# Four column groups of h side by side in the first chunk, paired transposes of x, and a later tanh, in a feed-forward kernel with its gradients

## The chip, the cores and the metric

One core of a Trainium2 chip runs the whole program. The metric is device time in microseconds (us), of the slowest core, which here is the only one. Before the change the time was 321.61 us, the median of 3 runs (321.59 to 321.71).

## The reference, cut to what matters

```python
B, S, D, F = 1, 2048, 640, 1536            # bfloat16
def _fwd_reference(x, w1, w2):
    h = jnp.einsum("bsd,df->bsf", x, w1)
    h = _silu(h)
    out = jnp.einsum("bsf,fd->bsd", h, w2)
    return out
# reference(): the output, and by jax.vjp the gradients of x, w1 and w2 for grad_out
```

The kernel does six products of the same size: h, the gradient at h ("g"), two products back to 640 columns ("out" and the gradient of x), and the two weight gradients. Each is 240 matmuls of 128x128 weights by 512 columns.

## The kernel before

The rows are worked in four chunks of 512. Only the start of the first chunk is touched by the change. Four 128-row tiles of x are loaded and transposed by TensorE through PSUM (the memory that takes TensorE's results); w1 is loaded in pieces, in the order of the columns that the first groups need; then twelve column groups of h follow, each of five matmuls (one for each 128-row slice of w1). Matmuls on a constant ("warm") precede, so that TensorE is busy while the loads run. After h comes the stage with w2.

```python
load_x_tile(nc.sync, 0); load_x_tile(nc.scalar, 1)         # 160 KB each
load_x_tile(nc.sync, 2); load_x_tile(nc.scalar, 3)
for lo, hi in ((0, 2), (2, DT)):                           # 128 KB, 192 KB: columns 0 to 255
    nc.sync.dma_start(out=w1_nat[:, lo:hi, 0:FH], in_=w1_v[:, lo:hi, 0:FH])
load_w1(FH, FC)                                            # 320 KB: columns 256 to 511
for fc in range(1, NFC):
    load_w1(fc * FC, (fc + 1) * FC)                        # 640 KB each
# ... (w2, transposed loads)
def pe_x_tile(xT, st):                                     # one tile of x, 5 transposes
    for lo, hi, copy in ((0, DS, nc.vector.tensor_copy), (DS, DT, nc.scalar.copy)):
        tp = ps_h.tile([P, hi - lo, P], dt_in, name="tp", tag="hp")
        for dt_ in range(lo, hi):
            nc.tensor.transpose(tp[:, dt_ - lo, :], x_nat[:, st, dt_ * P:(dt_ + 1) * P], ident[:])
        copy(out=xT[:, lo:hi, st * P:(st + 1) * P], in_=tp[:])

for st in range(STC):
    pe_x_tile(xT_next, st)
for i in range(NFILL):                                     # 4 fillers, behind the transposes
    nc.tensor.matmul(wp[:, 0:P], lhsT=ident[:], rhs=x_nat[:, STC - 1, 0:P], start=True, stop=True)

def h_group(ft, xT, aT, ghT):
    hp = ps_h.tile([P, SC], FP32, name="hp")               # one of 8 PSUM buffers
    for dt_ in range(DT):
        nc.tensor.matmul(hp[:], lhsT=w1_nat[:, dt_, ft * P:(ft + 1) * P], rhs=xT[:, dt_, :],
                         start=(dt_ == 0), stop=(dt_ == DT - 1))
    nc.scalar.activation(aT[:, ft, :], hp[:], ACT.Silu)
    # ... tanh of hp on ScalarE, then two VectorE steps
```

## Time and profile before

| what | before | view |
|---|---|---|
| time, 3 runs | 321.59 to 321.71 us | run times |
| time of the profiled run | 322.23 us (span 320.5) | run times, page |
| TensorE busy | 98% | page, part 1 |
| first h matmul | 6.48 us | timeline of PE |
| first matmul of the w2 stage | 19.43 us | timeline of PE |

From the page, the busy time of the engines and the chain that ended last (by engine, then by line; L161 is h, L196 the w2 stages). "PEld" is the weight loads, which overlap PE.

```profile
...
PE 314.0 (98%) x1477; PEld 145.9 (46%) x1506; DVE 101.8 (32%) x179; ACT 78.6 (25%) x142; POOL 0.7 (0%) x6
...
PE 97%; DMA 1%; issue 1%; ACT 0%; SPq 0%; DVE 0%; DVEq 0%
PE hp L196 32%; PE hp L180 16%; PE hp L286 16%; PE hp L161 16%; PE hp L334 15%; DMA x_nat<-in_x_dram 1%; PE hp L316 1%; ACT xT L149 0%; PE tp L148 0%; SPq L123 0%; DVE g_2366 L327 0%; DVEq L327 0%
...
```

From the timeline of TensorE, merged: start in us, length in us, line, operation, tiles, and in brackets the idle time before it and what ended it. L96 is the warm matmuls, L148 the transposes, L154 the fillers, L161 h, L196 the w2 stage.

```profile
...
0.78 2.93 PE L96 MATMUL wp<-const-bfloat16-1.0 128*128 128x128 bf16 x26 [0.78 <-PEq L362]
3.62 0.74 PE L148 MATMUL tp<-ident,x_nat 128*128 128x128 bf16 x10
5.32 0.73 PE L148 MATMUL tp<-ident,x_nat 128*128 128x128 bf16 x10 [0.96 <-DMA x_nat<-in_x_dram]
5.88 0.39 PE L154 MATMUL wp<-x_nat,ident 128*128 128x128 bf16 x4
6.48 13.11 PE L161 MATMUL hp<-xT,w_nat 128*128 128x512 bf16 x58 [0.21 <-ACT xT L149]
19.43 4.91 PE L196 MATMUL hp<-aT,w_nat 128*128 128x512 bf16 x22
```

All idling of TensorE lies ahead of 6.48 us, and the h stream then runs without a bracket. (A count of 58 and not 60 means two records missing in the trace.) From the waits of TensorE: total us, number, longest.

```profile
...
PE tp L148 <- DMA x_nat<-in_x_dram: 1.0, 1, 1.0
PE wp L96 <- PEq L362: 0.8, 1, 0.8
PE hp L161 <- ACT xT L149: 0.2, 1, 0.2
```

There is no fourth line: in the whole span TensorE waits three times.

### The profile page before, as it was taken

What the parts mean: (1) busy time and instruction counts of PE and PEld (TensorE: products, weight loads), DVE (VectorE), ACT (ScalarE), POOL (GpSimd) and SP (SyncE); (2) the same over time, 40 slices, a digit from 0 to 9 for tenths busy, and PEclk for the clock granted to TensorE, in tenths of its full rate; (3) what the DMA queues carried; (4) which work ended last, traced back from release to release, by engine and by line L of the source; (5) the groups of instructions that cost most, each with busy time, mean ns of one, the idle gap of its engine ahead of it and who ended that gap; (6) DMA issues with size and microseconds to landing.
All of it is one profiled execution on the core that took longest, in us unless ns stands there. A gap on an engine that the chain in (4) does not pass through costs nothing.

```text
span 320.5 us, 3556 instructions
## 1 busy us (share of the span) xinstructions
PE 314.0 (98%) x1477; PEld 145.9 (46%) x1506; DVE 101.8 (32%) x179; ACT 78.6 (25%) x142; POOL 0.7 (0%) x6
## 2 busy tenths in 40 slices
PE   7999999999999999999999999999999999999996
PEld 5444444444444444444444444444444444444443
DVE  1871551477510087810147741000000100001001
ACT  3960001555201255411054520110100001001100
POOL 0000000000000000000000000000000000000000
PEclk9999999999999999999999999999999999999999
DMA  8999999999699884392445079819999999995011
GB/s 246 316 192 209 254 265 253 320 271 277 215 229 336 203 237 122 118 319 66 127 159 141 2 254 268 217 25 293 262 240 263 249 203 343 251 281 181 33 49 35
DMA packets 149264, 66.69 MB, mean 208 GB/s; under 512 B 112640, under 2 KB 149248, under 8 KB 149248
## 3 DMA queue, kind: packets, MB, share of 16 engines
q1 hardware_dynamic: 148960, 66.13, 80.8%
q10 hardware_dynamic: 288, 0.33, 0.3%
q8 instruction: 12, 0.20, 0.2%
q14 instruction: 4, 0.03, 0.0%
HBM read 9.18 MB, written 28.97 MB: 119 GB/s over the span
## 4 chain that ended last, share of the span: by engine, by line
PE 97%; DMA 1%; issue 1%; ACT 0%; SPq 0%; DVE 0%; DVEq 0%
PE hp L196 32%; PE hp L180 16%; PE hp L286 16%; PE hp L161 16%; PE hp L334 15%; DMA x_nat<-in_x_dram 1%; PE hp L316 1%; ACT xT L149 0%; PE tp L148 0%; SPq L123 0%; DVE g_2366 L327 0%; DVEq L327 0%
## 5 line engine op out<-in xcount | busy, mean ns | idle before, releaser
L161 PE MATMUL hp<-xT,w_nat 128*128 128x512 bf16 x232 | 56.4, 379 | 0.6 <-ACT xT L149 0.2
L180 PE MATMUL hp<-goT,w2T 128*128 128x512 bf16 x238 | 56.8, 379 | 0.1
L196 PE MATMUL hp<-aT,w_nat 128*128 128x512 bf16 x235 | 52.2, 379 | 0.3
L196 PE MATMUL hp<-ghT,w1T 128*128 128x512 bf16 x235 | 52.2, 379 | 0.3
L286 PE MATMUL hp<-a_blk,go_nat 128*128 128x512 bf16 x236 | 51.8, 379 | 0.2
L334 PE MATMUL hp<-gh_blk,x_nat 128*128 128x512 bf16 x219 | 48.2, 379 | 0.3
L204 ACT ACTIVATE oT<-hp 128x512 bf16<-128x512 f32 x24 | 14.3, 597 | 110.0 <-PE hp L196 110.0
L168 ACT ACTIVATE aT<-hp 128x512 bf16<-128x512 f32 x48 | 28.7, 597 | 31.7 <-PE hp L161 31.7
L196 PEld LDWEIGHTS <-w_nat 128*128 128x128 bf16 x240 | 23.5, 98 | 28.3
L180 PEld LDWEIGHTS <-w2T 128*128 128x128 bf16 x240 | 23.5, 98 | 28.3
L286 PEld LDWEIGHTS <-go_nat 128*128 128x128 bf16 x240 | 23.5, 98 | 28.3
L161 PEld LDWEIGHTS <-w_nat 128*128 128x128 bf16 x240 | 23.4, 98 | 28.4 <-issue 0.4
L196 PEld LDWEIGHTS <-w1T 128*128 128x128 bf16 x240 | 23.4, 98 | 28.4
L206 DVE CAST oT<-hp 128x512 bf16<-128x512 f32 x16 | 11.1, 692 | 78.0 <-PE hp L196 78.0
L187 DVE SCALAR_TENSOR_TENSOR ghT<-ghT,hp 128x512 bf16<-128x512 bf16 x48 | 32.5, 682 | 7.3 <-PE hp L180 7.3
L334 PEld LDWEIGHTS <-x_nat 128*128 128x128 bf16 x224 | 21.9, 98 | 26.4
L173 DVE SCALAR_TENSOR_TENSOR ghT<-aT,v 128x512 bf16<-128x512 bf16 x48 | 33.0, 688 | 0.6
L172 DVE TENSOR_SCALAR v<-t 128x512 bf16<-128x512 f32 x48 | 20.5, 427 | 29.2 <-ACT t L170 29.2
L170 ACT ACTIVATE t<-hp 128x512 f32<-128x512 f32 x48 | 28.4, 591 | 0.0
L296 DVE CAST g2T<-hp 128x512 bf16<-128x512 f32 x7 | 4.8, 692 | 46.1 <-PE hp L286 46.1
L294 ACT ACTIVATE g2T<-hp 128x512 bf16<-128x512 f32 x8 | 4.8, 598 | 47.0 <-PE hp L286 40.7
L343 ACT ACTIVATE g_2140<-hp 128x512 bf16<-128x512 f32 x1 | 0.6, 597 | 13.6 <-DMA out_dram<-g_2077 13.6
(33 smaller groups left out, 29.3 us busy)
## 6 DMA issues: line engine op xcount, KB each, us to landing
aT_scr<-aT SPq DMA_DIRECT2D x4, 1536.0 KB, 6.7
ghT_scr<-ghT SPq DMA_DIRECT2D x4, 1536.0 KB, 8.0
out_dram<-o_sb SPq DMA_DIRECT2D x8, 640.0 KB, 3.4
oT_scr<-oT SPq DMA_DIRECT2D x4, 640.0 KB, 3.9
go_nat<-in_grad_out_dram SPq DMA_DIRECT2D x4, 640.0 KB, 8.1
gxT_scr<-oT SPq DMA_DIRECT2D x4, 640.0 KB, 4.7
w_nat<-in_w_dram SPq DMA_DIRECT2D x2, 960.0 KB, 10.9
x_nat<-in_x_dram SPq DMA_DIRECT2D x3, 640.0 KB, 7.8
```

The costliest lines, as they stand in the source:

```text
L161: nc.tensor.matmul(hp[:], lhsT=w1_nat[:, dt_, ft * P:(ft + 1) * P], rhs=xT[:, dt_, :], start=(dt_ == 0), stop=(dt_ == DT - 1),)
L168: nc.scalar.activation(aT[:, ft, :], hp[:], ACT.Silu)
L170: nc.scalar.activation(t[:], hp[:], ACT.Tanh, scale=0.5)
L172: nc.vector.tensor_scalar(out=v[:], in0=t[:], scalar1=-0.5, scalar2=0.5, op0=ALU.mult, op1=ALU.add)
L173: nc.vector.scalar_tensor_tensor(out=ghT[:, ft, :], in0=aT[:, ft, :], scalar=1.0, in1=v[:], op0=ALU.subtract, op1=ALU.mult)
L180: nc.tensor.matmul(gp[:], lhsT=w2T[:, dt_, ft * P:(ft + 1) * P], rhs=goT[:, dt_, :], start=(dt_ == 0), stop=(dt_ == DT - 1),)
L187: nc.vector.scalar_tensor_tensor(out=ghT[:, ft, :], in0=ghT[:, ft, :], scalar=1.0, in1=gp[:], op0=ALU.add, op1=ALU.mult)
L196: nc.tensor.matmul(op_[:], lhsT=w_all[:, ft, dt_ * P:(dt_ + 1) * P], rhs=rhs_all[:, ft, :], start=(ft == 0), stop=(ft == FT - 1),)
L204: nc.scalar.activation(oT[:, dt_, :], op_[:], ACT.Copy)
L206: nc.vector.tensor_copy(out=oT[:, dt_, :], in_=op_[:])
L286: nc.tensor.matmul(gp[:], lhsT=go_nat[:, st, dt_ * P:(dt_ + 1) * P], rhs=a_blk[:, st, :], start=(st == 0), stop=(st == ST - 1),)
L334: nc.tensor.matmul(gp[:], lhsT=x_nat[:, st, dt_ * P:(dt_ + 1) * P], rhs=gh_blk[:, st, :], start=(st == 0), stop=(st == ST - 1),)
```

## The change

The intent is to start the h stream earlier. Blocks of x are transposed for two tiles at once and copied block by block, so that the first 128-row block of all 512 rows is complete first. The first four groups then run side by side: slice 0 of w1 for groups 0 to 3, slice 1 for groups 0 to 3, and then what is left, group by group. This needs slice 0 of 512 columns first, so w1's first loads are cut by rows and not by columns, and the second one is issued from ScalarE's queue. The fillers move between the pairs in the source; in the built program they stand ahead of all transposes. Tanh of a group follows silu of the group three later, so that silu isn't held up when groups finish close together.

```diff
-        for lo, hi in ((0, 2), (2, DT)):
-            nc.sync.dma_start(out=w1_nat[:, lo:hi, 0:FH], in_=w1_v[:, lo:hi, 0:FH])
-        load_w1(FH, FC)
+        for eng, lo, hi in ((nc.sync, 0, 1), (nc.scalar, 1, 2), (nc.sync, 2, DT)):
+            eng.dma_start(out=w1_nat[:, lo:hi, 0:FC], in_=w1_v[:, lo:hi, 0:FC])
 ...
-        for st in range(STC):
-            pe_x_tile(xT_next, st)
+        def pe_x_pair(xT, st):
+            for dt_ in range(DT):
+                tp = ps_h.tile([P, 2, P], dt_in, name="tp", tag="hp")
+                for q in range(2):
+                    nc.tensor.transpose(tp[:, q, :], x_nat[:, st + q, dt_ * P:(dt_ + 1) * P], ident[:])
+                copy = nc.scalar.copy if dt_ % 2 else nc.vector.tensor_copy
+                copy(out=xT[:, dt_, st * P:(st + 2) * P], in_=tp[:])
+        pe_x_pair(xT_next, 0)
         for i in range(NFILL):
-            nc.tensor.matmul(wp[:, 0:P], lhsT=ident[:], rhs=x_nat[:, STC - 1, 0:P], ...)
+            nc.tensor.matmul(wp[:, 0:P], lhsT=warm, rhs=warm, start=True, stop=True)
+        pe_x_pair(xT_next, 2)
 ...
+        def h_first(xT, aT, ghT):                    # KM = 2, FB = 4, LAG_G = 3
+            hps = []
+            for ft in range(FB):
+                hps.append(ps_h.tile([P, SC], FP32, name="hp"))
+            for dt_ in range(KM):
+                for ft in range(FB):
+                    h_mm(hps[ft], ft, xT, dt_, dt_ + 1)
+            for i in range(FT + LAG_G):
+                if i < FT:
+                    if i < FB:
+                        h_mm(hps[i], i, xT, KM, DT)
+                    else:
+                        hps.append(ps_h.tile([P, SC], FP32, name="hp"))
+                        h_mm(hps[i], i, xT, 0, DT)
+                    silu_a(i, hps[i], aT)
+                if i >= LAG_G:
+                    silu_grad(i - LAG_G, hps[i - LAG_G], aT, ghT)
 ...
             if c == 0:
-                for ft in range(FT):
-                    h_group(ft, xT, aT, ghT)
+                h_first(xT, aT, ghT)
```

More of the change, by code (lines that the diff above doesn't have):

```diff
@@ L44 @@
     NFC = F // FC
+    FB = FC // P
     LAG = 2
+    LAG_G = 3
+    KM = 2
     NWARM = 26
@@ L114, in load_goT @@
             return goT
-        FH = FC // 2
         xT_next = xpool.tile([P, DT, SC], dt_in, name="xT")
@@ L140, with h_mm @@
         nc.sync.dma_start_transpose(out=w1T[:], in_=w1[:, :])
-        DS = 3
-        def pe_x_tile(xT, st):
-            for lo, hi, copy in ((0, DS, nc.vector.tensor_copy), (DS, DT, nc.scalar.copy)):
-                tp = ps_h.tile([P, hi - lo, P], dt_in, name="tp", tag="hp")
-                for dt_ in range(lo, hi):
-                    nc.tensor.transpose(tp[:, dt_ - lo, :], x_nat[:, st, dt_ * P:(dt_ + 1) * P], ident[:])
-                copy(out=xT[:, lo:hi, st * P:(st + 1) * P], in_=tp[:])
-        for st in range(STC):
-            pe_x_tile(xT_next, st)
-        for i in range(NFILL):
-            nc.tensor.matmul(
-                wp[:, 0:P], lhsT=ident[:], rhs=x_nat[:, STC - 1, 0:P], start=True, stop=True
-            )
-        def h_group(ft, xT, aT, ghT):
-            hp = ps_h.tile([P, SC], FP32, name="hp")
-            for dt_ in range(DT):
+        def pe_x_pair(xT, st):
[6 more added lines that the diff above has]
+        pe_x_pair(xT_next, 0)
+        for i in range(NFILL):
+            nc.tensor.matmul(wp[:, 0:P], lhsT=warm, rhs=warm, start=True, stop=True)
+        pe_x_pair(xT_next, 2)
+        def h_mm(hp, ft, xT, lo, hi):
+            for dt_ in range(lo, hi):
                 nc.tensor.matmul(
@@ L167, in h_group, with silu_a, silu_grad @@
                 )
+        def silu_a(ft, hp, aT):
             nc.scalar.activation(aT[:, ft, :], hp[:], ACT.Silu)
+        def silu_grad(ft, hp, aT, ghT):
             t = tpool.tile([P, SC], FP32, name="t")
@@ L175, in h_group @@
             )
+        def h_group(ft, xT, aT, ghT):
+            hp = ps_h.tile([P, SC], FP32, name="hp")
+            h_mm(hp, ft, xT, 0, DT)
+            silu_a(ft, hp, aT)
+            silu_grad(ft, hp, aT, ghT)
+        def h_first(xT, aT, ghT):
[15 more added lines that the diff above has]
+                    silu_grad(i - LAG_G, hps[i - LAG_G], aT, ghT)
         def g_group(ft, goT, ghT):
@@ L277 @@
         g2T_v = g2T_scr[:].rearrange("(dt p) f -> p dt f", p=P)
-        FB = FC // P
         k = 0
```

## The prediction

> **What bounds the kernel now.** TensorE. The page gives PE 98% busy; the chain of waits is 97% PE. In the timeline the first h matmul starts at 6.48 us; from there weight loads follow every 0.216 us to the end, with no gap over 0.24 us (1440 x 0.216 = 311 us, of a span of 320.5). The waits view has only three PE waits, all in the first 6.5 us: 0.8 at the start barrier, 1.0 for x, 0.2 for the last transposed copy. Besides, there are about 3 us of closing copy and store. So the change can only move the start of the h stream, or break its density.
>
> **The start today.** x tiles 0 and 1 land at 3.57 and 3.74 us, tiles 2 and 3 at 5.27 and 5.50. Ten transposes at a 56 ns pitch follow each pair. The last VectorE copy (3 blocks, 0.36 us) ends at 6.33, the last ScalarE copy at 6.46. The first w1 pieces land at 5.78, 6.43 and 7.39: none is late.
>
> **What the change does.**
> 1. Transposes pair two x tiles per 128-row block, block 0 first: x tile 3 lands 5.50, block 0 is transposed by about 5.77, its copy of 256 columns (estimate 0.29 us, from the 0.36 us of 384) done at about 6.10. Block 4's copy ends at about 6.5, as today, but is needed only 8 matmuls (1.73 us) after the start.
> 2. Four groups side by side: the same 240 matmuls, of which the first need only w1's first slice.
> 3. w1's first two slices (128 KB each) are issued on two queues. The Trainium skill, "DMA: Bandwidth & Descriptors", section "Issuing engines are not separate DMA queues", says such queues share the same 16 engines and interleave. So slice 0 shares bandwidth with slice 1: by bytes in front of it (estimate from today's landings: 768 KB by 5.78, 960 KB by 6.43) it lands near 6.1, about when block 0 is ready. The rest (1280 KB, 7.4 us) is needed at about 7.95. Thin, but it holds.
> 4. The four fillers are scheduled before the transposes (order of the built program), ending near 3.8; this doesn't delay the second pair.
> 5. Tanh trails silu by three groups. ScalarE needs 1.08 us per group, PE 1.08. The first four groups finish 0.65 us apart, so tanh catches up later. Eight PSUM buffers cover it. Worth nothing by itself: ScalarE never stalled PE.
>
> **On the critical path.** Only the start: from 6.48 to about 6.2-6.3 us (block 0 copied, slice 0 landed, 0.1 us of wait and weight load). The gain is 0.2 us, below 0.1%. Everything after shifts as a block.
>
> **Predicted:** 321.38 us, range 321.05 to 321.75; faster by over 2%: 0.003, within 2%: 0.99, slower: 0.007.
>
> **Shown right or wrong by:** the first h matmul in the timeline at 6.2-6.3; its releaser a w1 slice or a VectorE copy; no PE gap among the first 60 h matmuls; the span minus that start unchanged at 314.0.
>
> **What would make it wrong.** (a) Slice 0 or x tile 3 lands later, as queues share the engines: no gain. (b) The w1 rest lands after 7.95 and opens a gap. (c) The clock: "TensorE: Matmul & The Clock Gate", Part 1, tells of a clock that halves after idle windows. Today's clock record goes to full at 3.67 us and stays; losing it would add up to 1.7 us (half speed over one 3.4 us window, an estimate from that page). (d) PSUM is freed too late, as tanh lags: gaps at groups 8-11.

## The result

The changed kernel took 322.26 us (median of 4 runs, 321.92 to 322.62), beside 321.66 us before (median of 4, 321.59 to 321.77). The ratio is 1.0019, with a 95% interval of 1.0001 to 1.0036: the same, by a limit of 2%, and outside the predicted range of 321.05 to 321.75. (Ratios are the mean time of one kernel's runs over that of the other's of the same rounds, so not quite the ratio of the medians quoted.)

From the page of the changed kernel, the same lines. Line numbers moved: h is L158 now, the w2 stages are L221.

```profile
...
PE 314.9 (98%) x1477; PEld 147.0 (46%) x1506; DVE 101.7 (32%) x181; ACT 77.7 (24%) x142; POOL 0.7 (0%) x6
...
PE 96%; DMA 2%; issue 1%; SPq 0%; DVE 0%; DVEq 0%
PE hp L221 32%; PE hp L309 16%; PE hp L205 16%; PE hp L158 16%; PE hp L357 15%; DMA w_nat<-in_w_dram 2%; PE hp L339 1%; SPq L125 0%; SPq L132 0%; DVE g_2370 L350 0%; DVEq L350 0%
...
```

A load of w1 ("DMA w_nat") has come into the chain with 2% of the span; x has left it. From the timeline of TensorE (L153 fillers, L147 transposes, L158 h, L221 the w2 stage):

```profile
...
3.50 0.63 PE L153 MATMUL wp<-const-bfloat16-1.0 128*128 128x128 bf16 x4
3.93 2.29 PE L147 MATMUL tp<-ident,x_nat 128*128 128x128 bf16 x20
6.05 1.89 PE L158 MATMUL hp<-xT,w_nat 128*128 128x512 bf16 x7
8.58 11.40 PE L158 MATMUL hp<-xT,w_nat 128*128 128x512 bf16 x51 [0.64 <-DMA w_nat<-in_w_dram]
19.81 4.48 PE L221 MATMUL hp<-aT,w_nat 128*128 128x512 bf16 x20
```

The stream does start earlier, at 6.05 us against 6.48. But after eight matmuls (one record missing) it stops, and goes on at 8.58. The bracket says 0.64 us only, because the end of a matmul is drawn later than the time at which the next could start. At the pace of 0.216 us for each matmul, the ninth was due at 6.05 + 8 x 0.216 = 7.78; it came 0.80 us late. From the waits of TensorE:

```profile
...
PE wp L99 <- PEq L385: 0.8, 1, 0.8
PE hp L158 <- DMA w_nat<-in_w_dram: 0.6, 1, 0.6
```

The ninth matmul is the first that needs the 384 KB load with slices 2 to 4. From the list of DMA issues of the changed kernel, that load alone: line, queue, count, size, us from issue to landing.

```profile
...
w_nat<-in_w_dram SPq DMA_DIRECT2D x1, 384.0 KB, 6.4
```

It was issued at 2.12 us and landed 6.4 us later, at 8.53. In the kernel before, the load with the same number of bytes in front of it and in it (1280 KB with x) is this one:

```profile
...
w_nat<-in_w_dram SPq DMA_DIRECT2D x1, 320.0 KB, 4.8
```

It was issued at 2.63 us and landed at 7.39, more than a microsecond earlier, and was not needed until the eleventh matmul. The first reading was thus case (b) of the prediction's list, "the w1 rest lands after 7.95 and opens a gap". That is true of this run. Whether it is the cause of the difference is another question, and it took repeats to see it.

### The profile page after: what moved, and what is told of

Read it like the earlier page. It is cut to its first block, busy times and chain, and to the rows that moved or that the text cites. A ratio compares the mean times of both kernels' runs of the same rounds, so it can differ in the third digit from the quotient of the medians.

```text
span 320.9 us, 3558 instructions
## 1 busy us (share of the span) xinstructions
PE 314.9 (98%) x1477; PEld 147.0 (46%) x1506; DVE 101.7 (32%) x181; ACT 77.7 (24%) x142; POOL 0.7 (0%) x6
## 4 chain that ended last, share of the span: by engine, by line
PE 96%; DMA 2%; issue 1%; SPq 0%; DVE 0%; DVEq 0%
PE hp L221 32%; PE hp L309 16%; PE hp L205 16%; PE hp L158 16%; PE hp L357 15%; DMA w_nat<-in_w_dram 2%; PE hp L339 1%; SPq L125 0%; SPq L132 0%; DVE g_2370 L350 0%; DVEq L350 0%
## 5 line engine op out<-in xcount | busy, mean ns | idle before, releaser
L158 PE MATMUL hp<-xT,w_nat 128*128 128x512 bf16 x238 | 56.9, 379 | 0.7 <-DMA w_nat<-in_w_dram 0.6
L221 PE MATMUL hp<-ghT,w1T 128*128 128x512 bf16 x235 | 52.2, 379 | 0.3
L221 PE MATMUL hp<-aT,w_nat 128*128 128x512 bf16 x235 | 52.2, 379 | 0.3
L167 ACT ACTIVATE aT<-hp 128x512 bf16<-128x512 f32 x48 | 29.9, 625 | 33.4 <-PE hp L158 33.4
L158 PEld LDWEIGHTS <-w_nat 128*128 128x128 bf16 x240 | 23.4, 98 | 29.0 <-DMA w_nat<-in_w_dram 1.1
L221 PEld LDWEIGHTS <-w1T 128*128 128x128 bf16 x240 | 23.5, 98 | 28.3
L221 PEld LDWEIGHTS <-w_nat 128*128 128x128 bf16 x240 | 23.5, 98 | 28.3
L171 ACT ACTIVATE t<-hp 128x512 f32<-128x512 f32 x48 | 29.8, 625 | 0.0
L368 DVE CAST g_2081<-hp 128x512 bf16<-128x512 f32 x1 | 0.7, 692 | 9.7 <-PE hp L357 9.7
```

Source lines behind the costliest of these rows:

```text
L171: nc.scalar.activation(t[:], hp[:], ACT.Tanh, scale=0.5)
L221: nc.tensor.matmul(op_[:], lhsT=w_all[:, ft, dt_ * P:(dt_ + 1) * P], rhs=rhs_all[:, ft, :], start=(ft == 0), stop=(ft == FT - 1),)
```

## The experiments

These theories were put against each other. T0: the first profile of before was a late sample, so the prediction was anchored wrongly. T1: each load of w1 has a deadline, the matmul that first reads it; the change moves the deadline of the last 384 KB from the eleventh matmul to the ninth. T2: two queues with slices of w1 at once make the transfers lag. T3: the moved fillers, and the time at which the clock of TensorE goes to full, make the start late. T4: the trailing tanh holds something up. Where the texts speak of "303.0 us", the start of the w2 stage was taken at its first weight load, some 0.2 us ahead of its first matmul, which is used below. T-numbers, KM and LAG_G are as above. The runs were made in five groups, each with fresh or shared runs of before on the same chip.

### Both kernels again

No edit.

> The kernel before, once more, for a second profile of its start and for the noise. Theory T0 (the first profile was a late sample: 322.23 us, when the timed runs were 321.6): x tile 2 lands near 4.5 us and not 5.27, the h stream starts at 5.8 to 5.9 us and not 6.48, and the span is near 319.8. Rival (profiling itself adds 0.6 us): the start is at 6.4 to 6.5 again. Ratio 1.000 within 0.0005.

Measured: median 322.00 us of 6 runs (321.33 to 322.89); before's own 11 runs of the same rounds, 321.88 (321.54 to 322.28); ratio 1.0003 (0.9990 to 1.0016). The profiled run took 321.33. From its timeline of TensorE:

```profile
...
3.58 1.57 PE L148 MATMUL tp<-ident,x_nat 128*128 128x128 bf16 x20
4.98 0.39 PE L154 MATMUL wp<-x_nat,ident 128*128 128x128 bf16 x4
5.57 13.11 PE L161 MATMUL hp<-xT,w_nat 128*128 128x512 bf16 x60 [0.21 <-ACT xT L149]
18.52 5.78 PE L196 MATMUL hp<-aT,w_nat 128*128 128x512 bf16 x26
```

This is the same program as in the first profile, and its h stream starts at 5.57 us and not at 6.48. x tile 2 landed at 4.29 us instead of 5.27, so the twenty transposes run through without the idle 0.96 us. T0 is shown: the first profile was a late sample of a wide spread. (This one is early: 5.57, where 5.8 to 5.9 was expected.) Profiling shows no cost of its own: this profiled run was the quickest of the six, and the other five took 321.78 to 322.89. What made tile 2 late can be narrowed down. A load leaves sixteen completion marks in the trace, one for each of its parts. Tile 2 had the eighth at 4.01 us in the first profile and 4.03 in this one, the fifteenth at 4.56 and 4.25, the last at 5.27 and 4.29. Half of the load was as early in both; its slowest parts were not.

> The changed kernel, once more. T1 (the deadline): matmul 9 of the h stream waits for the 384 KB rest of w1's first columns; a PE gap of 0.3 to 0.9 us at that place again, time 322.0 to 322.5, and (end of stream) follows that landing. T3 (the clock went to full late, at 6.03 us): in a run where it goes to full before 4 us the gap vanishes and the time is 321.6 or less. Under chance alone (one slow transfer in one run) the ratio is 1.000.

Measured: median 322.10 us of 5 (321.60 to 322.40), ratio 1.0004 (0.9991 to 1.0017). The profiled run took 322.10. From its timeline of TensorE:

```profile
...
3.93 1.65 PE L147 MATMUL tp<-ident,x_nat 128*128 128x128 bf16 x20
6.23 13.12 PE L158 MATMUL hp<-xT,w_nat 128*128 128x512 bf16 x60 [0.65 <-DMA w_nat<-in_w_dram]
19.19 5.13 PE L221 MATMUL hp<-aT,w_nat 128*128 128x512 bf16 x23
```

There is no gap at the ninth matmul this time: the 384 KB landed at 7.18, ahead of 6.23 + 1.73 = 7.96. The stream waits at its start instead, for slice 0, which landed at 6.18. So T1's gap did not come again, while the time was as expected.

> The changed kernel on one more chip. T1: 0.1 to 0.6 us over before (pooled so far 0.35), the w2 stage of the profiled run starting at its time less 303.0. Chance: the mean of this one is at or under before's.

Measured: median 322.01 us of 5 (321.65 to 322.37); before on this chip 322.27 (321.76 to 322.67); ratio 0.9995 (0.9982 to 1.0008). The profiled run took 321.72. From its timeline of TensorE:

```profile
...
3.50 0.45 PE L153 MATMUL wp<-const-bfloat16-1.0 128*128 128x128 bf16 x4
3.79 1.51 PE L147 MATMUL tp<-ident,x_nat 128*128 128x128 bf16 x20
5.94 13.12 PE L158 MATMUL hp<-xT,w_nat 128*128 128x512 bf16 x60 [0.64 <-DMA w_nat<-in_w_dram]
18.90 5.34 PE L221 MATMUL hp<-aT,w_nat 128*128 128x512 bf16 x24
```

Again the wait is at the start, for slice 0 at 5.89, and there is no gap. Here the answer was "chance": the mean was at before's, a little under it. The transposes took 1.51 us for twenty, where the first profile of the changed kernel has 2.29 us: the clock record goes to full at 3.61 us here and at 6.03 there, and at half clock the pitch of a transpose (from one start to the next) is 107 ns and not 56. In "changed, again" the clock went to full at 4.69.

Put together, with landings from the trace (us from the start of the span; the time of the last of the sixteen completion marks of a load):

| profiled run | last x tile | first w1 piece | second | third (1280 KB with x) | h starts | w2 stage starts | time | time less w2 start |
|---|---|---|---|---|---|---|---|---|
| before, first | 5.50 | 5.78 | 6.43 | 7.39 | 6.48 | 19.43 | 322.23 | 302.80 |
| before, again | 4.64 | 5.19 | 5.85 | 6.95 | 5.57 | 18.52 | 321.33 | 302.81 |
| changed, first | 4.66 | 5.81 | 6.51 | 8.53 | 6.05 | 19.81 | 322.62 | 302.81 |
| changed, again | 4.54 | 6.18 | 5.99 | 7.18 | 6.23 | 19.19 | 322.10 | 302.91 |
| changed, third | 4.57 | 5.89 | 6.08 | 7.21 | 5.94 | 18.90 | 321.72 | 302.82 |

The last column is the main result. The time of a profiled run is the start of the w2 stage plus 302.8 us, in both kernels, to 0.1 us; the other fifteen profiles, variants included, give 302.65 to 302.98. Everything behind the first h stage is the same in length to that, so the differences between profiled runs are made before the w2 stage starts. For runs without a profile this is inferred. Their spans are on record, and in 134 of 138 runs the time is 1.72 to 2.06 us longer than the span; in four it is 2.24 to 2.80 (two of xsplit, one of each set without fillers, all below), and there part of the length lies outside the traced span. The scatter is large: before's 51 different runs have a mean of 321.97 us, a standard deviation of 0.32 us and go from 321.33 to 322.89. (Part of this lies between the chips: before's means on the five occasions run from 321.67 to 322.22 us, the lowest on the first.) The changed kernel's 14 runs have a mean of 322.10 us, a standard deviation of 0.31 us and go from 321.60 to 322.62. The ratios on three occasions were 1.0019, 1.0004 and 0.9995. No difference is shown.

### The deadline

`KM = 2` to `KM = 1`: only slice 0 is worked side by side, so the 384 KB are needed at the sixth matmul, with the same loads, queues, fillers and tanh.

> As changed, but side by side only for the first 128-row slice (KM 1): the rest of w1 is needed 5 matmuls (1.08 us) after the start, not 8 (1.73 us). Same loads, same queues, same fillers, same lag. T1: the gap grows by 0.65 us, and so does the time: 322.7 us (322.5 to 322.9). T2 and T3: no difference to the changed kernel.

Measured: median 322.71 us of 5 (322.29 to 322.94), on the same chip as "changed, again"; ratio to before 1.0023 (1.0011 to 1.0035). The mean is 0.59 us over that of the changed kernel in the same rounds, where 0.65 was expected. From the timeline of TensorE of its profiled run:

```profile
...
6.08 1.24 PE L158 MATMUL hp<-xT,w_nat 128*128 128x512 bf16 x5
8.13 12.04 PE L158 MATMUL hp<-xT,w_nat 128*128 128x512 bf16 x55 [0.82 <-DMA w_nat<-in_w_dram]
20.02 4.26 PE L221 MATMUL hp<-aT,w_nat 128*128 128x512 bf16 x19
```

Five matmuls, then the wait for w1, which landed at 8.09. This shows that the landing of the 384 KB binds in this run, with the deadline at the sixth matmul. With the deadline at the ninth, three profiles say that it binds in one run of three. Three more kept traces, lag0 and the two without fillers (below), have the same loads and the same deadline: there the 384 KB landed at 7.89, 7.95 and 7.58, in time each time. That makes one run in six (the landing of 8.09 in this run would have missed it too, at 6.08 + 1.73 = 7.81). So 0.59 is near 0.65 in part by luck: 0.65 takes the load to bind every time, while the seven landings with these loads (7.18 to 8.53), put against their own starts, give an estimate of 0.35 us on average and between 0 and 0.65.

The reverse dose loads the 384 KB as two halves by columns:

```diff
-(nc.sync, 2, DT)                       # columns 0 to 511
+(nc.sync, 2, DT, 0, FC // 2), (nc.sync, 2, DT, FC // 2, FC)
```

> As changed, but the 384 KB rest of w1's first 512 columns comes as two loads of 192 KB, columns 0 to 255 and 256 to 511. T1: matmul 9 waits for 1088 KB and not for 1280 KB, so the gap shrinks by 0.5 us or vanishes; 321.6 us or less (0.4 us under the changed kernel). T2 (the second queue makes transfers lag) and T3 (clock, fillers): no difference to the changed kernel, 322.1.

Measured: median 321.69 us of 5 (321.33 to 322.10), ratio 0.9995 (0.9983 to 1.0007); its mean was 0.32 us under the changed kernel's in the same rounds. The profiled run (322.10) has no gap in the stream, which starts late, at 6.34, waiting 0.81 us for slice 0. The direction is T1's and the size smaller, and with five runs each it is not outside the scatter.

### The queue, and smaller slices

Slice 1 on the first queue: `(nc.scalar, 1, 2)` to `(nc.sync, 1, 2)`.

> As changed, but w1's second slice goes out on the first queue, behind slice 0, and not on ScalarE's. T2 (two queues of w1 slices at once): in the trace the DMA rate of 4 to 5 us returns from 240-256 GB/s to about 319 (as in the kernel before), slice 0 lands near 5.2 to 5.4 us and not 5.8 to 6.3, its slowest engine lagging the median by less than 0.6 us; the time falls by 0.3 to 0.5 us against the changed kernel. Rival (the shape of the slices, 8 rows of 1 KB for each engine): rate and landing stay as in the changed kernel, time 322.1.

Measured: median 321.66 us of 5 (321.31 to 322.00), before 321.88, ratio 0.9996 (0.9983 to 1.0008). But slice 0 landed at 6.12 us and the DMA rate from 4 to 5 us was 220 GB/s, below the 240 and 252 of the changed kernel's first two profiles. So in this profile a slice lags without a second queue. One profile does not refute T2, though. Over all kept traces the eighth of slice 0's sixteen completion marks lies at 4.68 to 4.76 us in the three runs with both slices on one queue, and at 4.85 to 5.29 in the eight runs with slice 1 on the other queue; the last mark lies at 4.98 to 6.12 against 5.68 to 6.81. So half of slice 0 is there about 0.3 us later with the second queue, and the slowest parts scatter by more than that. No time here shows a gain from one queue, and the time of this run is within the scatter of before.

Both together (halves on one queue):

> As changed, with the rest of w1 in two halves and all w1 loads on one queue: both suspected costs undone. T1 and T2: start near 5.6, no gap after it, 0.3 to 0.5 us under before, about 321.4. If neither is the cause: 321.9 or more.

Measured: median 322.34 us of 5 (321.49 to 322.52), before 321.88, ratio 1.0011 (0.9998 to 1.0024). The profiled run, the quickest of the five, started its stream at 5.83 us and ran it without delay: the weight load of the 21st matmul, which reads the next 640 KB of w1, came 0.14 us later than the pace, at 10.07, but its matmul began at 10.14, where the pace has it. The others weren't profiled. The median is a miss for both theories, and not explained.

All five slices side by side, each a load of its own, on one queue (`KM = 5`):

> The change carried through: four groups side by side for all five slices, each slice (128 KB) its own load, all on one queue. T1: every slice has 0.86 us of work in front of the next, which takes 0.4 us to load, so only the start counts: near 5.6 us, no gap over 0.1 us at any slice, about 321.4. ScalarE gets four groups nearly at once and catches up; if PSUM then is short, gaps of some 0.1 us at groups 8 to 11.

Measured: median 322.51 us of 5 (322.15 to 323.61), ratio 1.0021 (1.0007 to 1.0035). From the timeline of TensorE of the profiled run, the slowest of the five (323.61):

```profile
...
5.74 4.48 PE L158 MATMUL hp<-xT,w_nat 128*128 128x512 bf16 x19
12.32 8.81 PE L158 MATMUL hp<-xT,w_nat 128*128 128x512 bf16 x39 [2.11 <-DMA w_nat<-in_w_dram]
...
```

The slices themselves held: twenty matmuls without a gap. The 21st reads the 640 KB of columns 512 to 1023, and these landed at 12.28 us, 8.0 us after their issue. From the view by windows: the stretch in us and its length, busy time of the engines, the granted clock, the busy share of the DMA engines and their rate in GB/s.

```profile
...
5.00:6.00 1.00, 0.98 (x14) 0.74 (x13) 0.91 (x5) 0.96 (x3) 0.00 (x0) 1.00 0.94 243
6.00:7.00 1.00, 0.97 (x5) 0.44 (x5) 0.08 (x1) 0.06 (x1) 0.00 (x0) 1.00 0.69 154
...
```

The rate fell to 154 GB/s between 6 and 7 us with the DMA engines busy for only 0.69 of it; in the first profile of before the same window has

```profile
...
6.00:7.00 1.00, 0.74 (x7) 0.41 (x6) 0.33 (x2) 0.46 (x2) 0.00 (x0) 1.00 1.06 316
...
```

So the deadline theory was right about the slices and had left out the next load. Why the rate fell is not settled: the fifth slice was issued only at 3.87 us, when one of x's first loads had landed (3.85), and the large load behind it at 4.24 (2.60 in the first profile of the changed kernel); it may be that the queue ran short. But the late issue alone does not make the gap. The large load had its eighth completion mark at 8.74 us, ahead of 10.06 where the 21st matmul was due, its fifteenth at 11.28 and its last at 12.28: here too the slowest parts made the wait.

### Tanh and the fillers

`LAG_G = 3` to `LAG_G = 0`:

> As changed, with silu and tanh of a group next to each other again (no trailing). Both theories: no difference to the changed kernel (322.1), no TensorE wait on ScalarE in the first 60 matmuls. Rival T4 (tanh's trailing holds PSUM too long or delays something later): faster by 0.2 us or more.

Measured: median 322.44 us of 5 (321.91 to 322.60), before 322.05, ratio 1.0010 (0.9998 to 1.0023). TensorE waits for ScalarE nowhere in the h stage of the profiled run. The trailing tanh neither costs nor gains anything that can be seen. (The changed kernel did not run in these rounds, so the two are compared through before only: 1.0010 beside the changed kernel's 1.0019, 1.0004 and 0.9995.)

`NFILL = 4` to `NFILL = 0` in the changed kernel, twice, on two chips:

> As changed, without its four fillers. T3 (the fillers, now ahead of the transposes, stand on the critical path where the clock goes to full late): transposes begin near 3.6 us and not 3.93, and runs bound by TensorE at half clock start 0.3 us earlier; on average 0.1 to 0.3 us less than the changed kernel, 321.8 to 322.0. If only w1's landings bound the start: no difference, 322.1.

> The changed kernel without fillers, once more. If the 0.7 us were scatter: within 0.3 us of before, as the changed kernel is (pooled 0.1 over before). If real: 0.5 us or more over before again; then the profile should show transposes starting near 3.7 us and a late w1 slice or a late clock behind the start.

Measured: median 322.64 us of 5 (322.37 to 323.26), ratio 1.0023 (1.0009 to 1.0036); again, 322.14 of 6 (321.75 to 322.94), ratio 1.0003 (0.9988 to 1.0017). The first result had an interval clear of 1, and would have made a story about fillers; the second took it back. T3 is not shown in either direction.

### Parts that might help

Paired transposes and moved fillers in the kernel before, with before's loads and order of groups:

> The kernel before with the paired transposes and the moved fillers alone; its w1 loads, its group-by-group h stream and its tanh order stay. T1/T2: w1a lands near 5.2, the stream starts 0 to 0.2 us earlier than before's 5.58 of the second profile; time 0.0 to 0.2 us under before. If the pairs or fillers (T3) cost the time, it is 0.3 us or more over before.

Measured: median 321.65 us of 5 (321.25 to 321.96), ratio 0.9992 (0.9980 to 1.0005). On another chip:

> Before with paired transposes and moved fillers, on one more chip. If the gain of 0.3 us was real: 0.1 to 0.4 us under before. If it was scatter: within 0.1 us of before, as pairs_nofill was.

Measured: median 321.61 us of 6 (321.21 to 322.73), ratio 0.9986 (0.9972 to 1.0000). Without fillers:

> The kernel before with paired transposes and no fillers. T3: 0.1 to 0.3 us under pairs (which was 0.3 under before), so 0.3 to 0.6 under before. Otherwise as pairs.

Measured: median 321.99 us of 5 (321.38 to 322.72), ratio 1.0002 (0.9989 to 1.0016). The pairs may be worth 0.1%; the intervals do not clear 1.

Now a version that takes the deadlines as its plan: before's loads by columns, paired transposes, two groups side by side for two slices and not four, no trailing of tanh (`LAG_G = 0`) and no fillers. The second piece of w1 (192 KB) is then needed at the fifth matmul instead of the third, and the third piece (320 KB) at the eleventh as before.

> A version to beat both: w1 loads as before (columns 0 to 255 in two pieces), paired transposes, no fillers, and only two groups side by side for two slices. T1: the second piece is needed 0.86 us after the start instead of 0.43, the third after 2.16 as before; so only x, the first piece and the transposes bound the start. 0 to 0.2 us under pairs_nofill, 0.3 to 0.7 us under before.

Measured: median 321.57 us of 5 (321.27 to 322.10), before 322.05, ratio 0.9990 (0.9978 to 1.0003). Its profile has weight loads late by 0.30 us at the fifth matmul and by 0.43 us at the 21st, the deadlines of the second and of the fourth load. The matmuls lose less, as a weight load has some time in hand (the first starts at 5.62 us, its matmul at 5.77): these two start 0.31 and 0.43 us after the ones before them instead of 0.216, and the whole stream lost 0.33 us (19.05 - 5.77 - 12.95). So the fourth load was cut in two as well, and the fillers put back:

```diff
-    NFILL = 0
+    NFILL = 4
-        for fc in range(1, NFC):
-            load_w1(fc * FC, (fc + 1) * FC)
+        load_w1(FC, FC + FC // 2)
+        load_w1(FC + FC // 2, 2 * FC)
+        for fc in range(2, NFC):
+            load_w1(fc * FC, (fc + 1) * FC)
```

> two_side with the four fillers back and w1's columns 512 to 1023 in two loads of 320 KB. T1: the gap of 0.43 us at matmul 21 (its wait for the 640 KB load) goes; 0.1 to 0.4 us under two_side, that is 0.4 to 0.7 us under before, 321.2 to 321.5. If landings are chance and nothing else: as two_side, 0.3 us under before.

> The version two_side_fc1 once more. If its gain is real: 0.3 to 0.6 us under before (ratio 0.998 to 0.999), the w2 stage of the profiled run starting between 18.0 and 18.6 us. If scatter: within 0.2 us of before.

Measured: median 321.75 us of 5 (321.45 to 322.08), before 322.27, ratio 0.9986 (0.9974 to 0.9998); again, 321.28 us of 4 (321.07 to 321.64), before 322.20, ratio 0.9972 (0.9959 to 0.9985). Both were on the same chip, and before's 12 runs of the second are the 11 of the first and one more. From the timeline of TensorE of the first profiled run (321.46):

```profile
...
3.91 0.72 PE L151 MATMUL tp<-ident,x_nat 128*128 128x128 bf16 x10
4.84 0.88 PE L151 MATMUL tp<-ident,x_nat 128*128 128x128 bf16 x10 [0.21 <-DMA x_nat<-in_x_dram]
5.66 13.11 PE L162 MATMUL hp<-xT,w_nat 128*128 128x512 bf16 x60
18.60 5.78 PE L225 MATMUL hp<-aT,w_nat 128*128 128x512 bf16 x26
```

Sixty matmuls without a bracket, from 5.66 us. The second profiled run (321.48) also has no gap in the stream, but starts it at 5.81 after a wait of 0.40 us for the first piece of w1, and its w2 stage at 18.77; 18.0 to 18.6 was expected. This version is 0.1 to 0.3% under before, clear of 1 both times, with runs of before that are mostly the same and so not two independent tests. Against the changed kernel it ran in the same rounds once: means of 321.75 and 321.98 us, which is not clear. What gave it the gain was not taken apart further.

The last one loads x by columns, so that two blocks of all four tiles come first (256 KB), then slices 0 and 1 (256 KB). It too has no fillers and no trailing tanh, and the later loads of w1 are cut in halves:

> x comes by columns: first 256 columns of all four tiles (256 KB), then w1's first two slices (256 KB), then the rest of x, then the rest of w1. The first 8 of 20 transposes and 8 matmuls need only 512 KB. T1: the h stream starts near 4.9 us, then waits for the rest of x and w1 at about 6.3 to 7; the w2 stage starts 0.4 to 0.8 us earlier than in before; 321.1 to 321.5. If the clock is at half then, the early matmuls take 0.43 us each and half of the gain is lost.

Measured: median 322.15 us of 6 (321.75 to 323.10), ratio 1.0002 (0.9987 to 1.0017). From the timeline of TensorE of the profiled run (321.86):

```profile
...
4.76 1.89 PE L160 MATMUL hp<-xT,w_nat 128*128 128x512 bf16 x8 [0.56 <-ACT xT L153]
6.48 0.83 PE L151 MATMUL tp<-ident,x_nat 128*128 128x128 bf16 x12
7.66 11.38 PE L160 MATMUL hp<-xT,w_nat 128*128 128x512 bf16 x52 [0.34 <-ACT xT L153]
18.88 5.34 PE L227 MATMUL hp<-aT,w_nat 128*128 128x512 bf16 x24
```

The stream starts at 4.76, as expected, but the other twelve transposes now stand inside it, 0.83 us long, and behind them a wait for the copy of the last block. In the kernel before, TensorE does this work while it waits for loads. The early start of about 1 us is given back in this run: 0.83 + 0.34 us. The time is a miss (321.1 to 321.5 was expected), but the median is worse than the stream: two of the six runs, 323.10 and 322.83, are 2.80 and 2.73 us longer than their spans. By spans the mean is 320.12 us, beside 320.41 for before in the same rounds. What those two runs spent outside the span is not known.

## Why the prediction was wrong

**The anchor: "The start today … 6.48" and "On the critical path. Only the start: from 6.48 to about 6.2-6.3 us" — the step that failed.** The start of 6.48 us belongs to a run of 322.23 us. The prediction subtracted the gain against this start from 321.61 us, the median of other runs. By the relation found here (time = start of the w2 stage + 302.8), a run of 321.61 us has its w2 stage at 18.8 us and so its h stream, if it runs without a gap, at about 18.8 - 12.95 = 5.9 us (60 x 0.216 = 12.95). Against that, a start at 6.2 to 6.3 is no gain at all. Put into the same relation, a start at 6.25 gives 6.25 + 12.95 + 302.8 = 322.0 us, where 321.38 was predicted, 322.26 was measured first, and the changed kernel's 14 runs have a mean of 322.10. By this estimate the anchor accounts for 0.6 of the 0.9 us of the miss. The other 0.3 is within the scatter, or the gap at the ninth matmul that one profile shows; these are not separated. The mismatch of 0.6 us between the profiled run and the recorded times was there to be seen before predicting.

**The range.** It was drawn as if the three recorded runs, 0.12 us apart, showed the scatter. Before's own runs have a standard deviation of 0.32 us, and only 14 of its 51 lie in the predicted range of 321.05 to 321.75. For the changed kernel it is 3 of 14.

**"The rest … is needed at about 7.95. Thin, but it holds."** Half right. The landing was estimated at 7.4 us; with the same loads it came at 8.53, 7.18 and 7.21. One profile of three, and one of six with these loads, missed the deadline, by 0.80 us of matmul pace. KM = 1 shows that this load can bind. The prediction used a point where a spread was needed.

**Slice 0 "lands near 6.1".** Right: 5.81, 6.18 and 5.89. **The start "at 6.2-6.3"**: 6.05, 6.23 and 5.94, right within the scatter, with a load of w1 as its releaser in two of three. The 6.05 of the first is in part luck: slice 0 had landed at 5.81, and the stream followed the last transpose (5.96), which the late clock had slowed. **"Span minus that start unchanged at 314.0"**: right for the two changed runs without a gap (320.2 - 6.23 = 314.0, 319.9 - 5.94 = 314.0).

**Fillers, tanh, PSUM.** Right: no wait of TensorE on ScalarE in the h stage, and lag0 as the changed kernel. **The clock** (c) was listed as a risk: it did come late in the first profile, at 6.03 us. It then slowed the transposes (2.29 us instead of 1.51), and the wait for the 384 KB hid that.

**The class** ("same", 0.99) was right: at 2% nothing changed. And the ratio of 1.0019 that made the prediction look refuted in its sign is, with ten more runs, a difference of 0.1 us against a scatter of 0.3. What the change gives (a first matmul that needs only one block of x and one slice) it pays for, in the runs where the 384 KB come late, with a tighter deadline for the next load.

## What to carry to other kernels

Before predicting a change of a few tenths of a microsecond, check that the profiled run and the timed runs agree; if they do not, find the one time in the trace from which the run time follows (here the start of the second stage plus a constant), and convert each timed run by it. Where a dense stream begins behind loads, write down for every load the matmul that first reads it and compare with the spread of landings over several profiles, not with one landing: moving the first deadline forward is worth nothing if the next load becomes the bound. A five-run mean in such a start phase can be off by half a microsecond, even with an interval clear of 1 (without fillers the mean was 0.73 us over before, and 0.13 when repeated); repeat before explaining.

## What the Trainium skill lacked or had wrong

- "TensorE: Matmul & The Clock Gate", Part 1, says that the clock goes to full about 4 us into sustained activity, give or take 500 ns. Here, with TensorE busy from 0.78 us in each run, the record goes to full at 3.61 to 3.67 us in some profiles (changed, third; both of before) and at 6.03 us (changed, first) or 6.64 us (pairs without fillers) in others, with more in between: 2.8 to 5.9 us into the activity, a spread of 3 us. The pitch of the transposes agrees with the record (107 ns up to 5.96 us in changed, first; 56 ns in changed, third). That the window runs free of the kernel, as the page says, fits this.
- The same page, Part 4, says that full clock does not engage for transposes and gives about 275 ns for one in a kernel. Here twenty transposes took 1.51 us at full clock (a pitch of 56 ns where they follow each other, each drawn 219 ns long) and 2.29 us at half clock (107 ns, 311 ns long). So full clock holds for transposes once it is there; whether transposes alone would bring it about is not shown.
- "DMA: Bandwidth & Descriptors", section "Why a DMA increments its semaphore by 16 and not by 1", says that a load is complete only when all its engines are. No figure is given of how far the slowest lags. In the first profile of the changed kernel the 384 KB load had its eighth completion mark at 6.38 us, its fifteenth at 7.92 and its last at 8.53; with the same loads again, 6.37, 7.00 and 7.18. The eighth marks are 0.01 us apart and the last 1.35: this lag, and not the rate of most of the load, made the gap. What makes it was not found here.
- The same page, section "Issuing engines are not separate DMA queues", says that loads issued from different engines run on the same 16 DMA engines and interleave; it is not at fault, as a second queue brought nothing sooner here. Slice 0 had half of its completion marks by 4.85 to 5.29 us with slice 1 on the other queue (eight traces), and by 4.68 to 4.76 with both on one (three traces), as sharing of the engines would have it.
